# The gated channel stage rewritten: keys of two token blocks by seven products, streamed key weights, transposed outputs

## The chip, the cores and the metric

One core of a Trainium2 chip runs the whole program. The metric is the device time of one execution in microseconds, as the median of repeated runs. The engines are TensorE (PE, with its weight loads as PEld), VectorE (DVE), ScalarE (ACT), GpSimd (POOL), and SyncE (SP), which issues all DMAs here. Each engine takes its instructions in program order.

## The reference

Eight batches of 576 tokens; eight heads of width 64. A retention layer (causal, with decay per head) feeds a channel mixer with a low-rank mix over the sequence, and its result feeds a second mixer, the gated stage, which the change rewrites:

```python
x = retention(q, k, v)                      # (8, 576, 512)
u = x + (x.T @ U @ V).T
x = u + np.maximum(u @ w_ch1, 0) @ w_ch2    # 512 -> 2048 -> 512
x_prev = shift_by_one_token(x)
xk = mu_k * x + (1 - mu_k) * x_prev
xr = mu_r * x + (1 - mu_r) * x_prev
k = np.maximum(xk @ w_k, 0.0)               # 512 -> 1024
v = k * k @ w_v                             # 1024 -> 512
out = v / (1 + np.exp(-(xr @ w_r)))
```

## The kernel before

Channels lie on partitions and tokens on the free axis, in 9 blocks of 512 tokens (`BT`). Every fp32 product is made of three fp32r matmuls: operands are split into a high part (a cast on ACT) and a low part (a subtraction), and high x high, low x high and high x low are summed in PSUM. A matmul is 128x128 stationary by 128x512 moving unless said otherwise.

The program has five stages. (1) Retention in 72 steps (`step_of`), with the first projection's tiles (`hidden`, `hidden_part`, L233) filled in between. Weights arrive as float64 words and are converted by lists of small steps (`convert`, `park`, `second_weight`); `slot` takes one step of each conversion under way and starts a new one where told, so these lists set where conversions stand in the queues of ACT, DVE, POOL and SP. The weights of the last stage are parked in DRAM. (2) The rest of the first projection; its results go to DRAM. (3) The second projection of blocks 0 to 7, in pairs (`products`, L405): 64 items, each loaded, summed (L345 to L350) and split (`split_item`, L364 and L365) one item ahead, 24 matmuls in the first half of a pair's items and 18 in the second. Two token blocks and four quarters of the weight are combined by seven products for eight. The converted weight `w2p`/`w2q` of item j must be there at item j. (4) The second projection of block 8 (`project`, L485 to L487), with the weights of the last stage fetched meanwhile. (5) The gated stage, L1048 on.

Up to stage 4 the order is written by hand (`tc.manual_schedule`, left at L1045). The gated stage is left to the scheduler, which takes `pump`'s background steps at a lower priority. It goes block by block: `shift_mix` makes xk and xr and splits them (16 shifts on ACT, L524; a mix on DVE, L533; a cast, L537; a subtraction, L539); `key_chunk` (8 per block, 12 matmuls each) evicts with a ReLU on ACT, squares on DVE from PSUM (L1067), casts (L1068) and subtracts on POOL (L1069); `gate_tile` (4 of 12) ends in a sigmoid on ACT (L1084); `value_tile` (4 of 24) has tokens on the output's partitions, is multiplied by the gate (L1099) and stored (L1101). `wk`, `wr` and `wv` stay in SBUF.

```python
    for t in range(NB):
        ...
        for f in range(DF2 // 128):
            key_chunk(t, f)
            pump(5)
        for i in range(4):
            gate_tile(t, i)
            pump(5)
        pump(1000)
        ...
        for i in range(4):
            value_tile(t, i)
            pump(6)
```

## Time and profile before

| | |
|---|---|
| median of 3 runs | 1406.4 us (1406.31 to 1408.29) |
| the profiled execution, its own time | 1404.54 us |
| its span in the profile | 1402.8 us |
| PE busy in the span | 1378.8 us, 98% |
| granted clock of TensorE, mean | 0.991 |
| DVE / ACT / POOL busy | 53% / 41% / 23% |
| moved by DMA | 244.67 MB, mean 174 GB/s |
| share of the chain that ended last: keys L1061, values L1095, gates L1080 | 14%, 14%, 7% |

The span is what the profiler's records cover; the time of an execution is 1.7 us longer. Ends of matmuls are modelled and overlap, so a busy PE is read together with the spacing of its matmuls in the chain. Some matmul records are missing, so counts come from the program.

### The profile page before, as it was taken

Reading aid. Unit: us, or ns where it says so; the run is one execution under the profiler, and the core shown is the slowest. Engines: PE = TensorE matmul, PEld = TensorE weight load, DVE = VectorE, ACT = ScalarE, POOL = GpSimd, SP = SyncE. Lnnn points to the kernel's source line nnn. Section 1 sums busy time; section 2 is a strip of 40 time slices with the busy share of each in tenths; the row PEclk is TensorE's granted clock in tenths of the full one; section 3 lists DMA queues with packets and bytes.
Section 4 is the critical chain, followed back from the end, with each engine's and each line's share of the span. In section 5 each row is a group of like instructions: output and inputs, shape, how many; then the busy total and the mean of one; then the engine's idle time right before and its main releaser. Section 6 shows DMA issues by size and latency. Waiting matters only on the chain.

```text
span 1402.8 us, 25526 instructions
## 1 busy us (share of the span) xinstructions
PE 1378.8 (98%) x10332; PEld 1122.2 (80%) x10332; DVE 741.2 (53%) x1145; ACT 580.5 (41%) x1019; POOL 325.3 (23%) x263
## 2 busy tenths in 40 slices
PE   6899999999999999999999999999999999999998
PEld 4677778777788887788888888888888888888887
DVE  5873545444451467798898976425324234234240
ACT  4542333333332445344444443434444344344440
POOL 3350221211220255022222222031121120120220
PEclk8899999999999999999999999999999999999999
DMA  9757576676752658779696967921011011010000
GB/s 344 257 201 236 189 277 237 226 268 208 260 189 110 218 187 288 260 234 323 220 314 217 313 238 234 393 78 61 23 38 61 16 45 61 16 46 30 8 23 30
DMA packets 98950, 244.67 MB, mean 174 GB/s; under 512 B 12816, under 2 KB 19344, under 8 KB 98832
## 3 DMA queue, kind: packets, MB, share of 16 engines
q1 hardware_dynamic: 98832, 243.04, 50.6%
q8 instruction: 81, 1.33, 0.4%
q14 instruction: 37, 0.30, 0.1%
HBM read 158.07 MB, written 84.93 MB: 173 GB/s over the span
## 4 chain that ended last, share of the span: by engine, by line
PE 96%; DVE 2%; DMA 1%; issue 1%; ACT 0%; SPq 0%; DVEq 0%; ACTq 0%
PE h L233 29%; PE k L1061 14%; PE v L1095 14%; PE r L1080 7%; PE gc L405 6%; PE ga L405 6%; PE gd L405 6%; PE gb L405 3%; PE up L605 2%; PE xn L705 2%; PE dn L658 1%; PE c L487 1%; PE c L486 1%; PE c L485 1%; PE up L630 1%; PE dn L646 1%
## 5 line engine op out<-in xcount | busy, mean ns | idle before, releaser
L239 ACT ACTIVATE hs<-h 128x512 f32<-128x512 f32 x144 | 86.0, 598 | 242.9 <-PE h L233 238.2
L1069 POOL TENSOR_TENSOR kl<-ks,kh 128x512 fp32r<-128x512 f32 x72 | 92.8, 1290 | 359.2 <-issue 241.9
L1099 DVE TENSOR_TENSOR o<-v,g 128x512 f32<-128x512 f32 x36 | 24.9, 692 | 187.2 <-PE v L1095 187.2
L1067 DVE SCALAR_TENSOR_TENSOR ks<-k,ka 128x512 f32<-128x512 f32 x72 | 49.6, 691 | 122.7 <-ACT ka L1065 67.7
L364 ACT CAST sbh<-rb 128x1024 fp32r<-128x1024 f32 x64 | 67.4, 1053 | 68.4 <-PE gd L405 56.5
L537 ACT CAST mh<-m 128x512 fp32r<-128x512 f32 x72 | 44.8, 622 | 118.4 <-DVE tp L530 82.7
L1095 PE MATMUL v<-wv_0u,kh 128*128 128x512 f32 x288 | 88.7, 389 | 0.0
L1095 PE MATMUL v<-wv_1u,kh 128*128 128x512 f32 x288 | 88.7, 389 | 0.0
L617 DVE TENSOR_TENSOR pm<-up,dtab 128x256 f32<-128x256 f32 x72 | 30.4, 422 | 108.5 <-PE up L630 91.4
L365 DVE TENSOR_TENSOR sbl<-rb,sbh 128x1024 fp32r<-128x1024 f32 x64 | 86.4, 1350 | 2.4 <-ACT sbh L364 2.2
L365 DVE TENSOR_TENSOR sal<-ra,sah 128x1024 fp32r<-128x1024 f32 (+1 forms) x64 | 67.1, 1048 | 24.5 <-PE gd L405 16.5
L364 ACT CAST sah<-ra 128x1024 fp32r<-128x1024 f32 (+1 forms) x64 | 53.5, 837 | 49.7 <-DVE ra L346 22.9
L1080 PE MATMUL r<-wru,mh 128*128 128x512 f32 x288 | 71.4, 389 | 0.0
L1061 PE MATMUL k<-mh,wk_0u 128*128 128x512 f32 x288 | 71.4, 389 | 0.0
L1061 PE MATMUL k<-mh,wk_1u 128*128 128x512 f32 x288 | 71.1, 389 | 0.0
L1068 ACT CAST kh<-ks 128x512 fp32r<-128x512 f32 x72 | 44.5, 621 | 55.5 <-DVE ks L1067 55.5
L1065 ACT ACTIVATE ka<-k 128x512 f32<-128x512 f32 x72 | 43.1, 598 | 50.6 <-PE k L1061 41.6
L1080 PEld LDWEIGHTS r<-wru,mh 128*128 128x128 f32 x288 | 54.0, 188 | 11.6 <-ACT g L1084 0.5
L1061 PEld LDWEIGHTS k<-mh,wk_0u 128*128 128x128 f32 x288 | 54.0, 188 | 11.4 <-DVE ks L1067 0.2
L1095 PEld LDWEIGHTS v<-wv_0u,kh 128*128 128x128 f32 x288 | 54.1, 188 | 11.3
L1061 PEld LDWEIGHTS k<-mh,wk_1u 128*128 128x128 f32 x288 | 54.1, 188 | 11.2
L1095 PEld LDWEIGHTS v<-wv_1u,kh 128*128 128x128 f32 x288 | 54.0, 188 | 11.2
(196 smaller groups left out, 3327.7 us busy)
## 6 DMA issues: line engine op xcount, KB each, us to landing
hp<-hs SPq DMA_DIRECT2D x128, 256.0 KB, 3.0
rb<-hp SPq DMA_DIRECT2D x64, 512.0 KB, 5.8
qk<-in_qk SPq DMA_DIRECT2D x32, 512.0 KB, 4.6
kv<-in_kv SPq DMA_DIRECT2D x32, 512.0 KB, 5.9
ra<-hp SPq DMA_DIRECT2D x32, 512.0 KB, 6.9
ur<-ub SPq DMA_DIRECT2D x18, 512.0 KB, 6.2
x2l<-xb SPq DMA_DIRECT2D x18, 512.0 KB, 5.2
out<-o SPq DMA_DIRECT2D x36, 256.0 KB, 2.0
```

Source lines behind the costliest of these rows:

```text
L233: nc.tensor.matmul(hps[t, f], w.part(lo, k, fo), u[k // 2][:, k % 2, :], start=(part == 0 and k == 0), stop=(part == 2 and k == KD - 1),)
L239: nc.scalar.activation(h, hps.pop((t, f)), AF.Relu)
L364: nc.scalar.copy(hi_, src)
L365: nc.vector.tensor_tensor(lo_, src, hi_.bitcast(F32), op=ALU.subtract)
L405: nc.tensor.matmul(group[g][p], l[:, col(p)], r, start=(h == 0 and j == 0 and i == 0), stop=(i == 2 and last), skip_group_check=True,)
L537: nc.scalar.copy(hk, m)
L1061: nc.tensor.matmul(ps, w.part(lo, k, fo), u[k // 2][:, k % 2, :], start=(i == 0), stop=(i == len(ops) - 1))
L1067: nc.vector.scalar_tensor_tensor(sq, ps, 0.0, a, op0=ALU.max, op1=ALU.mult)
L1068: nc.scalar.copy(kh, sq)
L1069: nc.gpsimd.tensor_tensor(kl, sq, kh.bitcast(F32), op=ALU.subtract)
L1080: nc.tensor.matmul(ps, x[k // 2][:, k % 2, io_], wr.part(lo, k), start=(j == 0), stop=(j == len(ops) - 1))
L1095: nc.tensor.matmul(ps, x[:, f % 2, io_], wv[f // 4].part(lo, f % 4), start=(j == 0), stop=(j == len(ops) - 1))
```

## The change

The gated stage goes by pairs of blocks (0 and 1, 2 and 3, 4 and 5, 6 and 7), block 8 alone, inside the hand order. What moves:

- *Keys by seven products.* For a pair and each of four groups g, the key weight's columns g and g+4 (of 8 tiles of 128), each in two halves of the 512 channels, form A11, A12, A21, A22, and the two blocks' halves X11, X21, X12, X22. `key_group` computes A11 X11, S3 T3, S1 T1, A12 X21, S2 T2, A22 T4, S4 X22 in four PSUM banks a, c, d, b, a, c, d: the last three accumulate onto the first, third and second bank after ACT has copied what stood there.
- *Key weights.* `key_weight` replaces the parks of `wk`: it forms S1 to S4 on POOL, splits all eight quarters and stores 2 MB per group. `load_keys` fetches a group (4 DMAs of 512 KB) ahead of its use, anew for every pair.
- *Preparation.* `prepare(q)` replaces `shift_mix`: xr of both blocks, then the seven X and T tiles with their splits. It is pumped three steps at a time in six value parts and eight gate tiles of the pairs' turn, six at a time in stage 4.
- *Transposed outputs, values per key group.* `value_part` adds one group's two tiles into four banks with output channels on partitions; the kernel's output is (512, 4608) and is transposed on the host. Gates are transposed too and held.
- *Elsewhere.* Two steps of retention (c of 4, batches 2 and 3) now take two hidden tiles instead of one; the last `second_weight` waits in `tick` and is started by `slot(2)` in the item loop; `SMALL` is 9, `cf` has 5 buffers.

```diff
@@ key_weight, new; load_keys, new
+        def sums():
...
+            nc.gpsimd.tensor_tensor(s1, a21, a22, op=ALU.add)
+            nc.gpsimd.tensor_tensor(s2, s1, a11, op=ALU.subtract)
+            nc.gpsimd.tensor_tensor(s3, a11, a21, op=ALU.subtract)
+            nc.gpsimd.tensor_tensor(s4, a12, s2, op=ALU.subtract)
...
+        return [
+            load, None, down, lambda: fill(0), lambda: fill(1), sums, lambda: parts(0),
+            lambda: store(0), lambda: parts(1), lambda: store(1),
+        ]
...
+    def load_keys(n):
+        for i, w in enumerate((wkp, wkq)):
+            w[n] = []
+            for lo in range(2):
+                x = big.tile([128, 4, 256], F32R, tag="unit", name=f"wk{n}_{i}{lo}")
+                nc.sync.dma_start(x.bitcast(F32), kept_k[n % NG][:, i, lo])
+                w[n].append(x)
@@ prepare, new; shift_mix goes
+        def split(nm, src):
...
+            nc.scalar.copy(h, src)
             yield
+            nc.vector.tensor_tensor(l, src, h.bitcast(F32), op=ALU.subtract)
             yield
...
+            yield from split("22", b[1])
...
+            nc.vector.tensor_tensor(t3, b[1], b[0], op=ALU.subtract)
             yield
+            yield from split("t3", t3)
+            nc.vector.tensor_tensor(b[0], b[0], a[0], op=ALU.subtract)
+            yield
+            yield from split("t1", b[0])
+            nc.vector.tensor_tensor(b[1], b[1], b[0], op=ALU.subtract)
+            yield
+            yield from split("t2", b[1])
+        yield from half(ts[0], 1)
+        yield from split("21", a[1])
+        if len(ts) == 2:
+            nc.vector.tensor_tensor(a[1], a[1], b[1], op=ALU.subtract)
+            yield
+            yield from split("t4", a[1])
@@ in the loops
+        for g in range(NG):
+            waiting.insert(4 * g, key_weight(g, big))
...
-            hidden(2 if b > 1 and c not in (4, 7) and i > 2 * NL + 1 else 1, False)
+            few = i < 2 * NL + 2 or c == 7 or c == 4 and b > 3
+            hidden(1 if few else 2, False)
...
-        slot(new=len(ticks) % 4 == 1)
+        slot(new=len(ticks) % 4 == 1 and len(waiting) > 1)
...
-        if waiting or going:
-            tick()
+        if n:
+            slot(2)
@@ square and key_group, new
+    def square(t, g, i, x, eng):
...
+        nc.vector.scalar_tensor_tensor(x, x, 0.0, x, op0=ALU.max, op1=ALU.mult)
+        nc.scalar.copy(h, x)
+        eng.tensor_tensor(l, x, h.bitcast(F32), op=ALU.subtract)
...
+        for m in (1, 7, 5, 2, 6, 4, 3):
...
+            if m in (1, 7, 5, 6):
+                kept[m] = small(F32, f"m{m}_{n}")
+                nc.scalar.copy(kept[m], ps[b])
+            elif m == 2:
+                nc.vector.tensor_tensor(kept[1], ps[b], kept[1], op=ALU.add)
+                square(te, g, 0, kept[1], nc.gpsimd)
+                nc.vector.tensor_tensor(kept[7], kept[7], kept[5], op=ALU.add)
+            else:
+                t, i = ((te, 1), (to, 0))[m == 3]
+                x = small(F32, f"c{m}_{n}")
+                nc.vector.tensor_tensor(x, ps[b], kept[6], op=ALU.add)
+                square(t, g, i, x, nc.gpsimd)
+                if m == 3:
+                    nc.vector.tensor_tensor(kept[7], kept[7], kept[6], op=ALU.add)
+                    square(to, g, 1, kept[7], nc.gpsimd)
@@ the stage's loop, new (a pair)
+            for o in range(KD):
+                gate_tile(t, o, (mine, other)[x])
+                pump(3)
...
+        pump(1000)
...
+            for g in range(NG):
+                n = q * NG + g
+                if g + 1 < NG:
+                    load_keys(n + 1)
...
+                key_group(n, mine)
+                if g > 0:
+                    if g == NG - 1:
...
+                        load_keys(n + 1)
+                        background.append(prepare(q + 1))
+                        PUMP[0] = 3
+                    value_part(ts[0], g - 1, other)
+            value_part(ts[0], NG - 1, other)
+            for g in range(NG):
+                value_part(ts[1], g, mine)
```

Three places in the programs, row by row. First DVE at the entry of stage 3, before: `w2f7`, `w2p7` and `w2q7` belong to the last weight's conversion, `rb`/`ra` are an item's sums, `sal` and `sbl` its splits (with ACT's casts `sah`, `sbh`).

```order
L281 TENSOR_SCALAR w2f7_6947<-w2a7_6924 128x512
L284 SCALAR_TENSOR_TENSOR w2f7_6947<-w2a7_6924,w2f7_6947 128x512
L287 SCALAR_TENSOR_TENSOR w2f7_6947<-w2raw7_1_6873,w2f7_6947 128x512
L365 TENSOR_TENSOR sbl0_6978<-rb0_6849,sbh0_6977 128x1024
L365 TENSOR_TENSOR sal0_6982<-ra0_6848,sah0_6981 128x1024
L345 TENSOR_TENSOR rb1_6897<-rb1_6897,ra1_6896 128x512
L346 TENSOR_TENSOR ra1_6896<-ra1_6896 128x512
L315 TENSOR_TENSOR w2p7_1_7030<-w2f7_6947,w2p7_0_7029 128x512
L315 TENSOR_TENSOR w2q7_1_7032<-w2f7_6947,w2q7_0_7031 128x512
L345 TENSOR_TENSOR rb2_6952<-rb2_6952,ra2_6951 128x512
L346 TENSOR_TENSOR ra2_6951<-ra2_6951 128x512
L365 TENSOR_TENSOR sal1_7049<-ra1_6896,sah1_7048 128x1024
```

All of it stands ahead of the sums and splits of items 1 and 2. The same conversion in the change, three items later:

```order
L457 TENSOR_TENSOR sal3_7182<-ra3_7057,sah3_7181 128x1024
L457 TENSOR_TENSOR sbl3_7186<-rb3_7058,sbh3_7185 128x1024
L373 TENSOR_SCALAR w2f7_7216<-w2a7_7213 128x512
L376 SCALAR_TENSOR_TENSOR w2f7_7216<-w2a7_7213,w2f7_7216 128x512
L379 SCALAR_TENSOR_TENSOR w2f7_7216<-w2raw7_0_7170,w2f7_7216 128x512
L437 TENSOR_TENSOR rb5_7132<-rb5_7132,ra5_7131 128x512
L438 TENSOR_TENSOR ra5_7131<-ra5_7131 128x512
L457 TENSOR_TENSOR sal4_7228<-ra4_7084,sah4_7227 128x1024
L457 TENSOR_TENSOR sbl4_7232<-rb4_7085,sbh4_7231 128x1024
L373 TENSOR_SCALAR w2f7_7216<-w2a7_7213 128x512
L376 SCALAR_TENSOR_TENSOR w2f7_7216<-w2a7_7213,w2f7_7216 128x512
L379 SCALAR_TENSOR_TENSOR w2f7_7216<-w2raw7_1_7172,w2f7_7216 128x512
```

The first of its three groups now stands between the split of item 3 and the sums of item 5, the second between the split of item 4 and the sums of item 6; the subtractions follow behind the split of item 5. Item 1 has none of it ahead.

Second, PE at the turn to block 1, before: whole key chunks `k`, twelve matmuls per output tile.

```order
L1061 MATMUL k1_0_10354<-mh1_0_0_10192,wk_0u00_9641 128x512 x2
L1061 MATMUL k1_0_10354<-mh1_0_1_10193,wk_0u10_9645 128x512 x2
L1061 MATMUL k1_0_10354<-mh1_0_0_10192,wk_0u01_9643 128x512 x2
L1061 MATMUL k1_0_10354<-mh1_0_1_10193,wk_0u11_9647 128x512 x2
L1061 MATMUL k1_0_10354<-ml1_0_0_10194,wk_0u00_9641 128x512 x2
L1061 MATMUL k1_0_10354<-ml1_0_1_10195,wk_0u10_9645 128x512 x2
L1061 MATMUL k1_1_10373<-mh1_0_0_10192,wk_0u00_9641 128x512 x2
L1061 MATMUL k1_1_10373<-mh1_0_1_10193,wk_0u10_9645 128x512 x2
```

And in the change at the turn to the second pair: `ka` and `kc` are banks of group 4 (the first of that pair), `wk4` its streamed weights.

```order
L1207 MATMUL ka4_11035<-kh11_1_10812,wk4_00_10586 128x512
L1207 MATMUL ka4_11035<-kh11_1_10812,wk4_01_10588 128x512
L1207 MATMUL ka4_11035<-kl11_1_10813,wk4_00_10586 128x512
L1207 MATMUL ka4_11035<-kh11_1_10812,wk4_00_10586 128x512
L1207 MATMUL ka4_11035<-kh11_1_10812,wk4_01_10588 128x512
L1207 MATMUL ka4_11035<-kl11_1_10813,wk4_00_10586 128x512
L1207 MATMUL kc4_11037<-kht3_1_10907,wk4_00_10586 128x512
L1207 MATMUL kc4_11037<-kht3_1_10907,wk4_01_10588 128x512
L1207 MATMUL kc4_11037<-klt3_1_10908,wk4_00_10586 128x512
L1207 MATMUL kc4_11037<-kht3_1_10907,wk4_00_10586 128x512
L1207 MATMUL kc4_11037<-kht3_1_10907,wk4_01_10588 128x512
L1207 MATMUL kc4_11037<-klt3_1_10908,wk4_00_10586 128x512
```

A product has six matmuls, and the bank `ka` is used again four products later.

Third, DVE at that turn, before: the last mixes and splits of block 1 and the first squares `ks` of its key chunks.

```order
L530 MEMSET tp1_1_2_10332 128x1
L533 SCALAR_TENSOR_TENSOR m1_1_2_10336<-x2l1_1_9941,mu_93,tp1_1_2_10332 128x512
L530 MEMSET tp1_1_3_10340 128x1
L533 SCALAR_TENSOR_TENSOR m1_1_3_10344<-x2l1_1_9941,mu_93,tp1_1_3_10340 128x512
L539 TENSOR_TENSOR ml1_1_1_10287<-m1_1_2_10336,mh1_1_1_10285 128x512
L539 TENSOR_TENSOR ml1_1_1_10287<-m1_1_3_10344,mh1_1_1_10285 128x512
L1067 SCALAR_TENSOR_TENSOR ks1_0_10369<-k1_0_10354,ka1_0_10367 128x512
L1067 SCALAR_TENSOR_TENSOR ks1_1_10388<-k1_1_10373,ka1_1_10386 128x512
```

In the change, the end of the pair's preparation and the start of its first key group (`x2l2`, `x2l3` are blocks 2 and 3, mixed in place; `klt2`, `kl21`, `klt4` low parts; `m1`, `m7`, `c4` what ACT or DVE took from the banks):

```order
L648 TENSOR_TENSOR klt2_1_10947<-x2l3_1_10292,kht2_1_10946 128x1024
L616 MEMSET tp2_0_2_10965 128x1
L620 SCALAR_TENSOR_TENSOR x2l2_1_10288<-x2l2_1_10288,mu_97,tp2_0_2_10965 128x512
L616 MEMSET tp2_0_3_10984 128x1
L620 SCALAR_TENSOR_TENSOR x2l2_1_10288<-x2l2_1_10288,mu_97,tp2_0_3_10984 128x512
L648 TENSOR_TENSOR kl21_1_10990<-x2l2_1_10288,kh21_1_10989 128x1024
L680 TENSOR_TENSOR x2l2_1_10288<-x2l2_1_10288,x2l3_1_10292 128x1024
L648 TENSOR_TENSOR klt4_1_11010<-x2l2_1_10288,kht4_1_11009 128x1024
L1215 TENSOR_TENSOR m1_4_11045<-kb4_11036,m1_4_11045 128x512
L1186 SCALAR_TENSOR_TENSOR m1_4_11045<-m1_4_11045 128x512
L1217 TENSOR_TENSOR m7_4_11053<-m7_4_11053,m5_4_11061 128x512
L1221 TENSOR_TENSOR c4_4_11090<-kc4_11037,m6_4_11082 128x512
```

The first group's additions and squares stand directly behind the split of T4 in DVE's queue.

## Rows read from the trace of the kernel before

**Rows 1.** The page, part 1: busy time, share and instructions by engine.

```profile
PE 1378.8 (98%) x10332; PEld 1122.2 (80%) x10332; DVE 741.2 (53%) x1145; ACT 580.5 (41%) x1019; POOL 325.3 (23%) x263
```

**Rows 2.** Busy time by stretch: us, engines, PEclk, DMA share, GB/s.

```profile
424.60:492.50 67.90, 67.90 (x413) 55.51 (x410) 23.33 (x39) 27.22 (x50) 12.57 (x13) 1.00 0.49 169
552.00:620.00 68.00, 64.31 (x275) 52.20 (x275) 57.21 (x60) 31.28 (x42) 19.12 (x12) 0.97 0.72 239
864.70:916.00 51.30, 51.30 (x227) 42.19 (x226) 23.67 (x35) 17.79 (x30) 8.88 (x7) 1.00 0.91 328
916.00:1400.00 484.00, 482.83 (x2129) 399.00 (x2127) 164.77 (x295) 199.45 (x371) 93.34 (x75) 1.00 0.11 37
```

**Rows 3.** The chain that ended last, 480 to 920 us: start, us, what.

```profile
479.92 71.64 PE h L233 x316
...
907.26 3.40 PE k L1061 x15
```

**Rows 4.** Waits of PE: in total, times, longest us.

```profile
PE ga L405 <- DVE sal L365: 4.4, 4, 3.2
...
PE gb L405 <- DVE sbl L365: 0.5, 1, 0.5
```

**Rows 5.** The chain, 552 to 575 us.

```profile
553.31 1.68 DVE sal L365
560.27 2.30 DVE sal L365
562.61 2.07 PE ga L405 x4
564.68 1.83 PE gc L405 x6
```

**Rows 6.** Timeline of DVE, 536 to 580 us: start, us, instruction, idle before.

```profile
550.30 0.42 DVE L281 TENSOR_SCALAR w2f<-w2a 128x512 uint32<-128x512 uint32 x1
550.75 0.69 DVE L284 SCALAR_TENSOR_TENSOR w2f<-w2a,w2f 128x512 uint32<-128x512 uint32 x1
...
560.27 2.29 DVE L365 TENSOR_TENSOR sal<-ra,sah 128x1024 fp32r<-128x1024 f32 x1
...
566.08 1.22 DVE L365 TENSOR_TENSOR sal<-ra,sah 128x1024 fp32r<-128x1024 f32 x1
```

**Rows 7.** Timeline of POOL, 530 to 600 us.

```profile
534.63 1.29 POOL L315 TENSOR_TENSOR w2p<-w2s,w2p 128x512 fp32r<-128x512 f32 x1 [3.62 <-ACT w2p L314]
...
561.43 2.25 POOL L315 TENSOR_TENSOR w2q<-w2s,w2q 128x512 fp32r<-128x512 f32 x1
```

**Rows 8.** DMA issues, 900 to 1400 us, then 400 to 560: KB, us to landing.

```profile
x2l<-xb SPq DMA_DIRECT2D x16, 512.0 KB, 5.2
wv_1u<-wv_kept SPq DMA_DIRECT2D x3, 512.0 KB, 10.6
...
w2raw<-in_moe_w_ch SPq DMA_DIRECT2D x16, 512.0 KB, 4.7
```

**Rows 9.** Groups of ACT: count, busy us, mean ns, idle before, releaser.

```profile
L364 ACT CAST sbh<-rb 128x1024 fp32r<-128x1024 f32 x64 | 67.4, 1053 | 68.4 <-PE gd L405 56.5 <-DMA ra<-t 3.6 <-PE ga L405 2.9
L524 ACT ACTIVATE tp<-x2l,omu 128x511 f32<-128x511 f32 x72 | 51.5, 715 | 5.6 <-DMA x2l<-xb 5.6
L537 ACT CAST mh<-m 128x512 fp32r<-128x512 f32 x72 | 44.8, 622 | 118.4 <-DVE tp L530 82.7 <-DVE m L533 30.3 <-PE c L487 5.2
...
L1084 ACT ACTIVATE g<-r 128x512 f32<-128x512 f32 x36 | 21.5, 597 | 61.0 <-PE r L1080 60.9
...
L526 ACT ACTIVATE tp<-edge,omu 128x1 f32<-128x1 f32 x64 | 17.9, 279 | 0.0
```

**Rows 10.** Groups of POOL.

```profile
L1069 POOL TENSOR_TENSOR kl<-ks,kh 128x512 fp32r<-128x512 f32 x72 | 92.8, 1290 | 359.2 <-issue 241.9 <-ACT kh L1068 117.3
...
L296 POOL TENSOR_TENSOR w2s<-w2f 128x256 f32<-128x256 f32 x8 | 6.8, 850 | 41.1 <-DVE w2f L287 41.1
```

**Rows 11.** Groups of DVE.

```profile
L533 DVE SCALAR_TENSOR_TENSOR m<-x2l,mu,tp 128x512 f32<-128x512 f32 x72 | 53.7, 751 | 13.5 <-ACT tp L524 6.5
L1067 DVE SCALAR_TENSOR_TENSOR ks<-k,ka 128x512 f32<-128x512 f32 x72 | 49.6, 691 | 122.7 <-ACT ka L1065 67.7 <-POOL kl L1069 54.9
...
L1099 DVE TENSOR_TENSOR o<-v,g 128x512 f32<-128x512 f32 x36 | 24.9, 692 | 187.2 <-PE v L1095 187.2
```

**Rows 12.** Timeline, 1398 to 1403 us: the end.

```profile
1399.00 0.69 DVE L1099 TENSOR_TENSOR o<-v,g 128x512 f32<-128x512 f32 x1 [4.79 <-PE v L1095]
```

More of the change, by code (lines that the diff above doesn't have):

```diff
@@ new lines, in key_tile @@
+    def key_tile(t, g, i, b):
+        n = NB // 2 * NG + g
+        w = (wkp, wkq)[i][n]
+        ps = bank(b, f"k{t}_{g}_{i}")
+        ops = [(k, l, r) for k in range(KD) for l, r in ((0, 0), (1, 0), (0, 1))]
+        for j, (k, l, r) in enumerate(ops):
+            x = xk[NB // 2, ("11", "21")[k // 2]]
+            nc.tensor.matmul(
+                ps, w[l][:, k // 2, col(k % 2)], x[r][:, k % 2, :],
+                start=(j == 0), stop=(j == len(ops) - 1),
+            )
+        a = small(F32, f"ka{g}_{i}")
+        nc.scalar.copy(a, ps)
+        square(t, g, i, a, nc.vector)
@@ new lines, in value_part @@
+    def value_part(t, g, base):
+        if g == 0:
+            vacc[t] = [bank(base + o, f"v{t}_{o}") for o in range(KD)]
+        kh, kl = kk.pop((t, g))
+        for i in range(2):
+            w = wv[i]
+            for o in range(KD):
+                for j, (lo, x) in enumerate(((0, kh), (1, kh), (0, kl))):
+                    nc.tensor.matmul(
+                        vacc[t][o], w.part(lo, g, col(o)), x[:, i, :],
+                        start=(g == 0 and i == 0 and j == 0),
+                        stop=(g == NG - 1 and i == 1 and j == 2),
+                    )
+            pump(PUMP[0])
+        if g == NG - 1:
+            for o in range(KD):
+                x = small(F32, f"o{t}_{o}")
+                nc.vector.tensor_tensor(x, vacc[t][o], gate[t, o // 2][:, o % 2, :], op=ALU.mult)
+                nc.sync.dma_start(io["out"][col(o), t * BT:(t + 1) * BT], x)
@@ L1029, in retention_mixer_kernel @@
         if p == 5:
-            load_u(NB - 1, big2)
-        if p == 1:
-            load_x2(0, big2)
-            background.append(shift_mix(0, 0, big))
-            background.append(shift_mix(0, 1, big))
-        for _ in range(2):
-            if p > 0 and fetches:
-                w, i = fetches.pop(0)
-                w.load(big, i)
-        pump(4)
-    finish(NB - 1)
-    while fetches:
-        w, i = fetches.pop(0)
-        w.load(big, i)
-    pump(1000)
-    order.__exit__(None, None, None)
```

292 lines of the change are left out of this document (193 added, 99 removed).

## The prediction

> **What bounds the kernel now.** I read the page's busy times first, then the windows by stage, then the chain, then the waits of PE. TensorE is busy 98% of the span [rows 1]. In the gated stage (916 to 1400 us) it is busy 482.8 of 484.0 us at a granted clock of 1.00, while DVE has work for 165, ACT for 199 and POOL for 93 us, and the DMA engines are used 11% [rows 2]. So a wait must show in PE itself to cost anything there, and whatever PE no longer computes is time. The chain prices one matmul: 316 of them in 71.64 us and 15 in 3.40 us, both 226.7 ns [rows 3]. PE's own longest wait since the start is at the entry of the second-projection stage: 3.2 us on DVE's split `sal` [rows 4]. The slice 552 to 620 is the only later one with PE visibly short of its time, 64.3 of 68.0 us at clock 0.97 [rows 2].
>
> **The matmuls.** Before, one block's gated stage is 96 key, 48 gate and 96 value matmuls. For a pair of blocks the keys are 192. After, a pair takes 4 groups x 7 products x 2 halves x 3 split terms = 168, as the order of PE shows (5436 matmuls of 128x512 before, 5340 now). Four pairs save 4 x 24 = 96 matmuls; gates, values and block 8 keep theirs. 96 x 226.7 ns = **21.8 us**, all of it on PE, which is the path [rows 2, 3]. The new matmuls have the same tile (128x128 stationary, 128x512 moving) so I take the same price.
> The Trainium skill (TensorE: Matmul & The Clock Gate, section Back-to-back issue gap) puts a sustained stream of weight load and matmul at about 131 ns for 512 columns. By that figure the 96 would be worth an estimated 12.6 us and the time would be some 9 us above my forecast; the rows of this case do not agree with it, and the sum goes by them.
>
> **The moved weight conversion.** `second_weight(7)` used to be converted just ahead of the first product; now its three DVE groups stand behind the splits of items 3, 4 and 5. Before, this crowd cost PE 0.5 + 3.2 us of waiting, and after the wait 4 matmuls took 2.07 and 6 took 1.83 us where 0.91 and 1.36 are the rule [rows 4, 5]: 1.6 us more, 5.3 in all. Without the conversion's 0.4 + 0.7 + 0.7 us (twice, [rows 6]) and its two subtractions, `sal` of item 1 comes some 4 us earlier and the old wait is nearly gone. But the work is paid later: an item's products last 24 x 0.2267 = 5.4 us, DVE's own part of an item is 2 x 0.69 + 2 x 1.22 = 3.8 us, so 1.6 us is free per item, and the conversion needs 5.0 us plus what POOL's share of it slows: a split of 1.22 us took 2.29 while POOL subtracted, and POOL's 1.29 became 2.25 [rows 6, 7]. Its raw weights are also read later, behind the item loads (4.7 us to landing [rows 8]), and ACT and DVE stand still in order until they are there. The bounds are 5.3 us saved and, if the same crowd waits twice, 5.3 lost. I take **1.0 saved**, since the free time of items 3 to 6 (6.5 us) is about what the conversion and its slowing need.
>
> **Key weights, converted and streamed.** Before, `wk` is converted by 8 parks; now by 4 key conversions: as many DVE groups, 8 more casts on ACT (0.62 us each), 16 sums (0.85) and 8 more subtractions (1.29) on POOL [rows 9, 10]. They lie beside the recurrence and the first projection, where the slice of the same kind of conversion shows PE busy 67.9 of 67.9 us [rows 2]. I take 0; if the cover went, one wait like the longest on record, 3 us. In the gated stage each group fetches 4 x 512 KB, issued one group ahead: 2 MB against 9.5 us of products (14.9 with a value part). At the 328 GB/s of the slice 864.7 to 916 [rows 2] that is 6.4 us; 512 KB landed in 5.2 us singly and 10.6 in a crowd [rows 8]. Cost 0; at the far end 10.6 - 9.5 = 1.1 us at the first group of four pairs, 4.4 us. At the stage's entry 12 loads (6.3 MB, 19 us) are queued after the last projection, and the second group's key is due 21.8 + 9.5 = 31 us later: hidden.
>
> **Preparation of the next pair.** This is the one place where PE can be made to wait on a chain. `prepare(q+1)` starts behind key group 3, is spread over six value parts and eight gate tiles (240 matmuls, 54.4 us), and its last piece, T4, is due at the sixth product, 30 matmuls or 6.8 us later. ACT needs 16 x (0.715 + 0.279) + 8 x 0.622 + 7 x 1.053 = 28.3 us, DVE 16 x 0.75 + 8 x 0.69 + 11 x 1.22 = 30.9 [rows 6, 9, 11]; 8 sigmoids (4.8) and 8 output products (5.5) share the queues. Each engine alone fits easily. But the end (split 22, T3, T1, T2, split 21, T4) hands one tile to and fro: sum 1.22, cast 1.05, split 1.22, four times 3.5 and twice 2.3, plus two mixes: 21 us without gaps, some 24 with the sigmoids that fall into it. It begins behind the first gate tile (2.7 us) and its sigmoid (0.6), so ACT copies the first key product, behind it in its queue, at about 27.5; PE reuses that bank 21.8 + 5.4 = 27.2 us after the gate tiles began. I take **0.5 us for each of three pairs, 1.5**. The first pair's preparation has seven projection steps as well, and block 8 has no pair.
>
> **Key groups among themselves.** ACT copies four products (0.6 each), DVE does nine operations of 0.69, POOL four of 1.29 per group [rows 9 to 11]: 6.2 and 5.2 us beside 9.5. The last product of a group ends at 9.5; its bank is read by 10.5 and overwritten at 12.2 by the next group. Margin 1.7, cost 0.
>
> **The end.** Last matmul, one product of 0.69 us, one store [rows 12]. Now four stores come 0.68 us apart, each 256 KB, which at 328 GB/s needs 0.80: **0.4 us** more.
>
> **Sum**, against the profiled execution's own 1404.5 us: -21.8 - 1.0 + 1.5 + 0.4 = -20.9, giving 1383.6. The median of the runs shown is 1406.4, 1.9 above that execution, so the forecast is **1385.5 us**. What a measurement of this kernel can tell from no change is about 0.2%, 2.8 us.
>
> **The rivals.**
> A. *The late conversion costs nothing*: the DVE lead of items 1 to 3 swallows it. For it: 1.6 us free per item. Against: POOL's slowing. 5.3 saved in place of 1.0: 1381.2.
> B. *The key weights come late* at the first group of each pair, as in the crowd of 10.6 us [rows 8]. Against: only 11% DMA use in that stage. 4.4 us: 1389.9.
> C. *DVE and POOL exclude each other* inside the key groups. For it: 2.29 and 2.25 us side by side against 1.22 and 1.29 alone [rows 6, 7]; before, the squares of this stage ran at 0.69 because they read PSUM [rows 11], while four squares a group now read SBUF twice. Two blockings of 1.29 in a group exceed the margin of 1.7 by 0.9; 16 groups give 14 us: 1399.9. Against: the bank reads themselves keep one PSUM source.
> The Trainium skill (SBUF — State Buffer, section Who interferes with whom) states that a DVE instruction with two SBUF inputs and a GpSimd one that reads SBUF exclude each other for a whole instruction. By that rule the squares wait and the bank reads do so only behind them; the rows at 560 us agree with it.
> D. *Slower*: the preparation chain of a pair runs with no overlap between ACT and DVE. Then 28.3 + 30.9 + 4.8 + 5.5 = 69.5 us must pass in 54.4 + 6.8 = 61.2: 8.3 us of PE waiting at the first key group of three pairs, each followed by the 1.6 us of slow matmuls seen after a wait [rows 5]. 3 x 9.9 = 29.7 in place of 1.5: 1413.7, slower by 0.5%. It decides from about 5.7 us of wait per pair upward. For it: one generator, each step needing the last; against: for the first half (the eight gate splits) the next shift runs on ACT while DVE subtracts, so overlap is built in.
>
> **How the numbers follow.** Forecast 0.70 (its own range 1381 to 1392), A 0.08, B 0.07, C 0.07, D 0.08. Of D about a quarter is a half-exposed chain that lands within 2.8 us of before. So faster 0.92, same 0.02, slower 0.06. The range goes from 1380, just under A, to 1397, above B and over the half of C where fewer groups are blocked; D and the worst of C are left out, some 12 in 100, the rest being uncertainty within the forecast (the 5.3 us lost, the 3 us of the early stage).
>
> **What would show it.** Right: 96 fewer matmul records of 128x512, 226.7 ns apart; a gated stage some 21 us shorter with PE waits under 3 us in it; the waits on `sal` no longer at item 1 but small ones at items 4 to 6; the first key product of pairs 1 to 3 waiting about half a microsecond on ACT. Wrong: PE waiting for `wk` loads (B), DVE squares of 1.3 us or more and waits at bank d (C), waits of 5 us and more with a lower granted clock at three places 103 us apart (D), or a matmul spacing other than 226.7 ns.

## The result and the profile after

The changed kernel takes 1394.55 us (median of 4 runs, 1392.13 to 1395.8) beside 1406.45 us for the kernel before (1406.31 to 1408.29): a ratio of 0.991 with a 95% interval of 0.9893 to 0.9927, so 11.9 us faster. The forecast was 1385.5 us, 20.9 us faster, in a range of 1380 to 1397. The sign is right and the time lies in the range, near its upper end: 9 us of the expected gain are missing.

The page of the changed kernel, part 1, answers to [rows 1]: 96 matmuls fewer, as counted, while DVE has gained 115 us of work and is still far from PE.

```profile
span 1393.3 us, 25624 instructions
...
PE 1359.9 (98%) x10236; PEld 1103.6 (79%) x10236; DVE 856.2 (61%) x1243; ACT 589.1 (42%) x1021; POOL 353.2 (25%) x279
```

The time of PE between points that both programs share tells where it went. The points are the fifth transpose `xn` of the retention stage (called the recurrence from here on), the first product of the second projection (`ga` to `gd`), the first gate matmul, the last matmul. All are starts on PE's timeline, in us; 36 key matmuls of the kernel before lie ahead of its first gate matmul, and their 8.2 us (36 x 226.7 ns) are counted in the gated stage.

| stretch | before | after | difference | the prediction's term |
|---|---|---|---|---|
| start to fifth `xn` | 36.1 | 38.6 | +2.5 | 1.9 (own time against median) |
| fifth `xn` to first product | 516.2 | 523.1 | **+6.9** | 0, at most 3 |
| first product to first gate | 356.4 | 355.5 | -0.9 | -1.0 |
| gated stage to last matmul | 489.8 | 471.5 | **-18.3** | -21.8 + 1.5 |
| last matmul to the end | 4.3 | 4.7 | +0.4 | +0.4 |
| span | 1402.8 | 1393.3 | -9.4 | -20.9 |

Two lines are off: the recurrence lost 6.9 us where nothing was forecast, and the gated stage won 2.0 us less than forecast. Both show in PE's own waits, which answer to [rows 4].

```profile
PE xn L850 <- ACT xs L860: 5.0, 3, 1.8
...
PE ga L497 <- DVE sal L457: 3.4, 3, 2.1
PE ka L1207 <- ACT m L1213: 2.7, 4, 0.7
```

**In the recurrence** PE now waits three times for ACT's eviction `xs`, in chunks 3, 4 and 5. (The 72 steps go through eight sequences of nine steps and five transposes each; these are the chunks, numbered from 0.) In the kernel before PE is busy through the whole of such a stretch. The busy times by stretch, first of the kernel before, then of the changed kernel for the two chunks and for the stretches that answer to [rows 2]; the columns are those named there.

```profile
190.00:250.00 60.00, 60.00 (x806) 47.94 (x806) 28.40 (x57) 21.46 (x41) 12.15 (x11) 1.00 0.70 243
250.00:310.00 60.00, 60.00 (x806) 47.91 (x806) 28.39 (x57) 21.46 (x41) 12.14 (x11) 1.00 0.69 234
```

```profile
200.00:262.00 62.00, 60.38 (x806) 47.99 (x805) 28.48 (x60) 23.71 (x45) 19.06 (x18) 1.00 0.79 268
262.00:323.00 61.00, 59.41 (x802) 47.19 (x801) 27.55 (x60) 23.69 (x45) 18.10 (x17) 1.00 0.80 268
561.70:630.00 68.30, 64.86 (x281) 52.01 (x280) 61.80 (x64) 32.53 (x43) 22.57 (x14) 1.00 0.76 255
917.20:1388.90 471.70, 469.04 (x2065) 386.96 (x2063) 280.57 (x379) 196.67 (x351) 98.24 (x68) 1.00 0.37 130
```

PE lacks 1.6 us in each of the two chunks, at a DMA share of 0.79 and 0.80 instead of 0.70 and 0.69. DVE has no more work than before, ACT 2 us more and POOL 6 to 7 us more. The timelines of SP, ACT and PE around the first of these waits show what is late.

```profile
188.00 1.40 SPq L275 DMA_DIRECT2D keys<-wkl  x2
194.63 0.33 SPq L712 DMA_DIRECT2D qk<-in_qk  x1
...
197.94 1.16 SPq L179 DMA_DIRECT2D wr_raw<-in_moe_w_r  x1
```

```profile
205.47 0.66 ACT L104 ACTIVATE ca<-wr_raw 128x512 f32<-128x512 f32 x1 [7.45 <-DMA wr_raw<-in_moe_w_r]
206.04 0.57 ACT L860 COPY xs<-xn 128x512 f32<-128x512 f32 x1
```

```profile
204.62 0.41 PE L803 MATMUL dn<-pm,kv 64*64 64x64 f32 x16
206.66 0.63 PE L850 MATMUL xn<-ident,xt 128*64 128x128 f32 x4 [1.62 <-ACT xs L860]
```

Behind the key stores SP issues nothing from 189.4 to 194.6 us. In the trace the second of these stores, asked for at 187.18 us, lands at 194.56, and the load of `qk` is asked for at 194.63; the last one lands at 195.81, and the load of `kv` is asked for at 195.87. The raw weight that is queued behind is asked for at 197.9 and lands at 205.4; ACT, whose queue says to scale it now, stands 7.45 us; the eviction behind it is late, and PE waits. SP's waits in 200 to 323 us name what held it: buffers whose stores had not landed. In 190 to 310 us of the kernel before SP has no such wait on a store.

```profile
SPq L712 <- DMA keys<-wkh: 11.3, 2, 6.4
SPq L712 <- DMA wv_kept<-wv_0p: 3.5, 1, 3.5
SPq L714 <- DMA wr_kept<-wrp: 2.9, 1, 2.9
```

**In the gated stage** 96 gate matmuls run from 917.21 to 938.97 us, 226.7 ns each, as forecast. The only waits are the four of 0.7 us at `ka`, one in each pair. With the restart behind it each loses 0.9 to 1.0 us. They stand not at the first key group, where the preparation ends, but at the sixth product (the fifth in the order of issue) of the second key group. The first pair around that place, on PE, ACT, DVE and POOL:

```profile
953.70 0.39 PE L1207 MATMUL kb<-kl,wk 128*128 128x512 f32 x1
954.83 0.73 PE L1207 MATMUL ka<-kht,wk 128*128 128x512 f32 x2 [0.74 <-ACT m L1213]
```

```profile
950.27 0.62 ACT L1187 CAST vh<-c 128x512 fp32r<-128x512 f32 x1 [0.70 <-DVE c L1186]
953.67 0.62 ACT L1187 CAST vh<-m 128x512 fp32r<-128x512 f32 x1 [2.77 <-DVE m L1186]
954.20 0.58 ACT L1213 COPY m<-ka 128x512 f32<-128x512 f32 x1
```

```profile
949.55 0.69 DVE L1186 SCALAR_TENSOR_TENSOR c<-c 128x512 f32<-128x512 f32 x1
950.16 1.78 DVE L1224 TENSOR_TENSOR m<-m,m 128x512 f32<-128x512 f32 x1
951.98 1.66 DVE L1186 SCALAR_TENSOR_TENSOR m<-m 128x512 f32<-128x512 f32 x1
```

```profile
949.65 3.45 POOL L1188 TENSOR_TENSOR vl<-c,vh 128x512 fp32r<-128x512 f32 x2 [1.47 <-ACT vh L1187]
```

While POOL makes its two subtractions DVE's last sum and square of the group take 1.78 and 1.66 us instead of 0.69, so ACT's cast of that square comes late, and behind it in ACT's queue stands the copy of the next group's first product, which frees bank a for that group's sixth product. All subtractions of this kind beside DVE (`vl<-c`) and the others (`vl<-m`), from the page, with their mean in ns:

```profile
L1188 POOL TENSOR_TENSOR vl<-m,vh 128x512 fp32r<-128x512 f32 x32 | 41.4, 1293 | 266.0 <-ACT vh L1187 241.1
L1188 POOL TENSOR_TENSOR vl<-c,vh 128x512 fp32r<-128x512 f32 x32 | 55.2, 1745 | 24.7 <-ACT vh L1187 24.7
```

In the later groups a value part of 5.4 us lies between, and nothing waits.

### The profile page after: what moved, and what is told of

Read it like the earlier page. It is cut to its first block, busy times and chain, and to the rows that moved or that the text cites. A ratio compares the mean times of both kernels' runs of the same rounds, so it can differ in the third digit from the quotient of the medians.

```text
span 1393.3 us, 25624 instructions
## 1 busy us (share of the span) xinstructions
PE 1359.9 (98%) x10236; PEld 1103.6 (79%) x10236; DVE 856.2 (61%) x1243; ACT 589.1 (42%) x1021; POOL 353.2 (25%) x279
## 4 chain that ended last, share of the span: by engine, by line
PE 85%; DVE 6%; DMA 6%; issue 2%; ACT 1%; SPq 0%; DVEq 0%; ACTq 0%
PE h L325 28%; PE v L1252 14%; PE r L1174 7%; PE gc L497 4%; PE gd L497 4%; PE ga L497 4%; PE ka L1207 3%; PE kc L1207 3%; PE kd L1207 3%; PE gb L497 2%; PE up L750 2%; PE k L1236 2%; PE kb L1207 2%; DVE sal L457 1%; PE xn L850 1%
## 5 line engine op out<-in xcount | busy, mean ns | idle before, releaser
L1174 PE MATMUL r<-rh,wru 128*128 128x512 f32 x288 | 88.6, 389 | 0.0
L1252 PE MATMUL v<-vh,wv_0u 128*128 128x512 f32 x288 | 88.6, 389 | 0.0
L1252 PE MATMUL v<-vh,wv_1u 128*128 128x512 f32 x288 | 88.6, 389 | 0.0
L1174 PEld LDWEIGHTS r<-rh,wru 128*128 128x128 f32 x288 | 54.1, 188 | 11.2
L1252 PEld LDWEIGHTS v<-vh,wv_0u 128*128 128x128 f32 x288 | 54.1, 188 | 11.2
L1252 PEld LDWEIGHTS v<-vh,wv_1u 128*128 128x128 f32 x288 | 54.1, 188 | 11.2
L1188 POOL TENSOR_TENSOR vl<-c,vh 128x512 fp32r<-128x512 f32 x32 | 55.2, 1745 | 24.7 <-ACT vh L1187 24.7
L1174 PE MATMUL r<-rl,wru 128*128 128x512 f32 x144 | 56.0, 389 | 0.0
L1252 PE MATMUL v<-vl,wv_0u 128*128 128x512 f32 x144 | 56.0, 389 | 0.0
L1252 PE MATMUL v<-vl,wv_1u 128*128 128x512 f32 x144 | 56.0, 389 | 0.0
```

Of the source, the lines that this page charges most:

```text
L1174: nc.tensor.matmul(ps, wr.part(lo, k, col(o)), x[k // 2][:, k % 2, :], start=(j == 0), stop=(j == len(ops) - 1),)
L1188: eng.tensor_tensor(l, x, h.bitcast(F32), op=ALU.subtract)
L1252: nc.tensor.matmul(vacc[t][o], w.part(lo, g, col(o)), x[:, i, :], start=(g == 0 and i == 0 and j == 0), stop=(g == NG - 1 and i == 1 and j ...
```

## The experiments

In the table the profiled execution of each kernel is cut at the same points. The middle columns are the recurrence from the fifth transpose to the first product, then the second projection, then the gated stage.

| kernel | median us | ratio, 95% interval | to fifth `xn` | to first product | to first gate | to last matmul |
|---|---|---|---|---|---|---|
| changed kernel | 1394.55 | 0.9893-0.9927 | 38.6 | 523.1 | 355.5 | 471.5 |
| late_down | 1394.89 | 0.9900-0.9925 | 38.2 | 522.9 | 355.9 | 471.5 |
| sum_early | 1394.62 | 0.9884-0.9912 | 38.8 | 526.4 | 355.7 | 469.1 |
| old_ticks | 1399.60 | 0.9933-0.9968 | 38.4 | 525.4 | 359.3 | 471.5 |
| one_store | 1393.95 | 0.9892-0.9917 | 38.9 | 521.9 | 355.8 | 471.6 |
| no_store | 1386.80 | 0.9844-0.9871 | 39.0 | 517.2 | 355.2 | 469.1 |
| keys_gap | 1386.91 | 0.9843-0.9870 | 37.3 | 518.5 | 355.2 | 469.1 |
| keys_late | 1405.80 | 0.9989-1.0006 | 38.8 | 535.5 | 356.5 | 469.5 |
| gap_only | 1389.75 | 0.9861-0.9891 | 38.6 | 518.0 | 356.3 | 471.5 |
| gap_old | 1391.59 | 0.9877-0.9906 | 39.5 | 519.7 | 359.3 | 469.1 |
| gap_spread | 1389.42 | 0.9856-0.9891 | 39.0 | 519.5 | 355.0 | 469.1 |
| bytes_only | 1386.61 | 0.9831-0.9873 | 36.9 | 518.4 | 356.0 | 469.1 |

**late_down: an empty slot ahead of ACT's scaling.**

```diff
-                waiting.append(convert(fetch, parts, 128, 512, store))
+                steps = convert(fetch, parts, 128, 512, store)
+                steps.insert(1, None)
+                waiting.append(steps)
```

> Edit: the conversion of each parked weight (`wr`, `wv`) gets one empty slot between the load of the raw words and ACT's scaling of them. Theory (ACT reads its queue in order and stands behind raw weights that SP, busy with the key stores, asks for late; the evictions `xs` behind it make PE wait 1.8 us at three places): the three waits of xn on xs, 5.0 us together, and their restarts go, the first product of the second projection comes some 5 us earlier, and the time is 1389 to 1391. Rival (the early loss comes from the other spread of the hidden first-projection tiles, two at step 4 of the first chunks): no change, 1393 to 1396. Rival (the load is simply too slow for any slot): the wait of ACT moves to the next slot, with another instruction behind it, and the time stays within 2 us of 1394.5.

No change in the time. The waits on `xs` at the transposes are gone, 5.0 us of them, but PE lost as much in other places: from the last transpose of chunk 3 to that of chunk 4 it takes 61.8 us, as the changed kernel does (59.9 before). Its waits between 140 and 335 us:

```profile
PE dn L793 <- POOL kv L723: 2.1, 2, 1.1
PE mx L903 <- ACT xs L862: 0.7, 3, 0.2
PE h L327 <- ACT hs L333: 0.2, 1, 0.2
```

So ACT's place in line was a symptom. With it out of the way PE waits for POOL's `kv`, the load of the next chunk; these waits are 3.0 us, and how the rest of the loss comes about was not taken apart. The time is also what the first rival forecast, the other spread of the hidden tiles; that rival falls with no_store, bytes_only and keys_gap below, which keep this spread and lose 1.0 to 2.4 us in the recurrence instead of 6.9.

**sum_early: the last sum and square of a key group made earlier.**

```diff
                 nc.scalar.copy(kept[m], ps[b])
+                if m == 6:
+                    nc.vector.tensor_tensor(kept[7], kept[7], kept[6], op=ALU.add)
+                    square(to, g, 1, kept[7], nc.gpsimd)
...
-                if m == 3:
-                    nc.vector.tensor_tensor(kept[7], kept[7], kept[6], op=ALU.add)
-                    square(to, g, 1, kept[7], nc.gpsimd)
```

> Edit: in a key group the seventh product's last sum and its square are made behind product 6 instead of last, so that the last square of a group is that of product 3. Theory (the four waits of 0.7 us at the sixth product of the second group of each pair come from ACT's copies standing behind the cast of the last square, which DVE makes in 1.8 + 1.7 us instead of 0.7 + 0.7 while POOL subtracts): these waits, 2.7 us, and the 0.3 us lost at each restart go, 3 to 4 us faster, 1390.5 to 1391.5. Rival (they are the end of the preparation chain, as forecast): the waits stay at pairs 2 to 4 and the time changes by less than 1 us.

The four waits on `ka` are gone, and the gated stage is 2.4 us shorter. Its profile has only one group of waits left from 560 us on:

```profile
PE ga L497 <- DVE sal L457: 4.1, 5, 2.0
```

Of the 0.9 to 1.0 us per pair 0.3 to 0.4 stay: by the spacing of the matmuls PE now loses them one product later, at bank c. The time did not follow in this pair of medians, because the recurrence, where the program is the same as in the changed kernel, took 526.4 us here and 523.1 there; the runs of this kernel spread from 1389.99 to 1396.49 us. keys_gap against gap_only, below, gives the same edit a time: 1386.91 against 1389.75, 2.8 us. The rival (the end of the preparation chain) falls: nothing of that chain was touched, and the wait stood in the first pair too.

**old_ticks: the last weight pair converted ahead of the first products again.**

```diff
-        slot(new=len(ticks) % 4 == 1 and len(waiting) > 1)
+        slot(new=len(ticks) % 4 == 1)
...
-        if n:
-            slot(2)
+        if waiting or going:
+            tick()
```

> Edit: the slots around the second projection as before the change (a new conversion at every fourth tick, ticks and not pairs of slots in the item loop), so that `second_weight(7)` is converted ahead of the first products again. By the prediction's term (moved conversion, 1.0 us saved) this is 1.0 us slower than the changed kernel, 1395 to 1396; the wait on `sal` at item 1 is back at some 3 us. Rival A (the late conversion costs nothing): 4 to 5 us slower, 1399. Rival (the same crowd waits twice, nothing saved): 0 to 4 us faster.

5.0 us slower, the time that rival A gave. Of it the second projection holds 3.8 us (359.3 against 355.5); the rest is the recurrence, which has the same program. To have the move without that noise it was repeated on keys_gap (gap_old).

**one_store: one DMA where two stored a part.**

```diff
-                for w in range(2):
-                    nc.sync.dma_start(
-                        kept_k[g][:, w, lo, 2 * i:2 * i + 2], x[:, 2 * w:2 * w + 2].bitcast(F32)
-                    )
+                nc.sync.dma_start(
+                    kept_k[g][:, :, lo, 2 * i:2 * i + 2],
+                    x.bitcast(F32).rearrange("p (w s) n -> p w s n", w=2),
+                )
```

> Edit: each part of the converted keys is stored by one DMA instead of two, 4 issues on SP per key group and not 8. Theory (SP's queue, crowded by the key stores of 0.6 to 0.7 us each, issues the raw weights late): the loads behind come 1.3 to 2.6 us sooner, the three waits on xs shrink by about half, 1 to 3 us faster, 1391.5 to 1393.5. Rival (the raw weights are late because SP waits for a store's data or a free buffer, and the number of issues is nothing): no change within 1 us, 1393.5 to 1395.5.

0.6 us, within the spread, and the waits on `xs` are 4.2 us in place of 5.0. The number of issues on SP is not it; the rival's time came.

**no_store and bytes_only: what of the store costs.** The first leaves the stores out, and the gated stage reads other words of the same number in their place; the second leaves the converted parts unstored and moves the same bytes from a table that holds no buffer of the conversions. Both have the early last sum.

```diff
-            lambda: store(0), lambda: parts(1), lambda: store(1),
+            None, lambda: parts(1),
...
-                nc.sync.dma_start(x.bitcast(F32), kept_k[n % NG][:, i, lo])
+                nc.sync.dma_start(
+                    x.bitcast(F32), wr.kept[:, :, lo, i * 256:(i + 1) * 256]
+                )
```

> Edit: the converted keys are not stored (this leaves out the 8.4 MB of key stores in the recurrence; the gated stage reads other words of the same number in their place), with the early last sum of sum_early in the gated stage. Theory (the chunks 3 to 5 of the recurrence lose some 1.8 us each because SP's loads of the next chunk wait for buffers whose key store has not landed, at a DMA share of 0.79 where it was 0.70 before, and ACT, DVE and POOL stand behind late loads): the waits of SP on key stores go, the DMA share of 200 to 330 us falls to about 0.72, PE waits for nothing there, and the first product of the second projection comes at 557 to 558 us, 5 us earlier; the time is 1385 to 1388. Rival (it is the arithmetic of the key conversion on ACT, DVE and POOL, 8 more casts, 16 sums and 8 more subtractions): the first product stays at 561 to 564 and the time at 1390 to 1392, the gain of the early sum alone.

```diff
-                        kept_k[g][:, w, lo, 2 * i:2 * i + 2], x[:, 2 * w:2 * w + 2].bitcast(F32)
+                        kept_k[g][:, w, lo, 2 * i:2 * i + 2],
+                        qtab[:, w].rearrange("p a i -> p (a i)").rearrange("p (s n) -> p s n", n=256)
```

> Edit: the key stores move the same bytes to the same places, but from a table that is always there (the factors of the queries) instead of from the converted parts, which this leaves unstored; so a part's buffers are free as soon as they are made. With the early last sum, to be set against no_store (no bytes, no buffers held) and sum_early (both). If the held buffers are the cause: first product of the second projection 517 to 519 us behind the fifth transpose, as in no_store (517.2), DMA share of 200 to 323 us still at 0.78 or more, time 1386 to 1388. If the bytes are the cause: 521 to 526 us, as in the changed kernel (523.1) and sum_early (526.4), PE waits on xs at chunks 3 to 5, time 1391 to 1395.

Both have the recurrence back: 517.2 and 518.4 us, where the kernel before takes 516.2 and the changed kernel 523.1. Busy times of the two chunks, first of no_store, then of bytes_only:

```profile
200.00:262.00 62.00, 62.00 (x814) 49.49 (x813) 29.39 (x60) 23.77 (x46) 20.60 (x19) 1.00 0.71 240
262.00:323.00 61.00, 61.00 (x810) 48.63 (x810) 30.71 (x66) 25.31 (x48) 19.22 (x17) 1.00 0.72 239
```

```profile
200.00:262.00 62.00, 62.00 (x814) 49.51 (x813) 27.76 (x61) 24.32 (x47) 18.60 (x17) 1.00 0.79 273
262.00:323.00 61.00, 60.79 (x808) 48.34 (x806) 27.99 (x63) 24.58 (x48) 18.60 (x17) 1.00 0.79 274
```

This separates the two things that were one in the theory. With all the bytes of the changed kernel on the DMA engines (0.79) PE waits for almost nothing, as long as no buffer is held by them. And the arithmetic of the conversion, still all there in both, costs PE 0.2 us at most in these two chunks. (bytes_only also frees the stores from waiting until a part is made; but in 200 to 323 us of the changed kernel SP's waits at its store line are 0.7 us in all, and none is for a part.) The loss is the time for which a converted part keeps its buffers until its store has landed, while SP's next load, in line, wants that buffer. What the 1.0 to 2.2 us are that stay above the kernel before was not taken apart.

**keys_gap, gap_only and keys_late: the same work, placed otherwise.** The first two leave a place of the sequence empty behind each key conversion (the first with the early last sum, the second without); the third puts the key conversions at places 9, 11, 13 and 15, with the early last sum.

```diff
-            waiting.insert(4 * g, key_weight(g, big))
+            waiting.insert(5 * g, key_weight(g, big))
+            waiting.insert(5 * g + 1, [None])
```

> Edit: behind each of the four key conversions in the recurrence one place of the sequence stays empty (two steps), so that the next raw weight is asked for later; with the early last sum. Theory (the crowd of bytes and buffers around each key conversion): the waits on xs shrink from 1.8 us to below 1 at each of three places, first product at 558 to 561, time 1387 to 1389.5. Rival (each key conversion costs its 1.8 us wherever it stands): first product at 562 to 566, time 1390 to 1392.

> Edit: the empty places behind the key conversions alone, without the early last sum. Theory (the two losses are separate: 5 to 6 us in the recurrence, 0.6 us a pair at the second key group): 2.4 us slower than keys_gap, 1389 to 1390, with the four waits on the copies of product 1 back and the gated stage at 471.5 us from first to last matmul. Rival (the early last sum gives nothing that shows in the time): 1386 to 1388.

Both as the theory said, keys_gap at the lower edge of its range: 518.5 and 518.0 us in the recurrence, and the waits of SP on stores in 200 to 323 us are gone. 1386.91 us is 7.6 us less than the changed kernel and 1.4 more than the forecast: it beats both kernels, at a ratio of 0.9857 to the kernel before. gap_only has the four waits back and 471.5 us of gated stage.

```diff
-            waiting.insert(4 * g, key_weight(g, big))
+            waiting.insert(8 + 2 * g, key_weight(g, big))
```

> Edit: the four key conversions stand at places 9, 11, 13 and 15 of the sequence instead of 1, 5, 9 and 13, so that they run in the last three chunks, where the DMA share of the changed kernel falls to 0.36; with the early last sum. Theory (bytes and buffers): the loss of chunks 3 and 4 goes, some is left where two conversions overlap in chunks 5 and 6; first product at 558 to 562, time 1386.5 to 1390. Rival (each key conversion costs 1.8 us wherever it stands): the loss only moves to the later chunks, first product at 562 to 566, time 1390 to 1392.

Both expectations fell: 1405.8 us, 11 us slower than the changed kernel. Chunks 3 and 4 are clean, as the theory had it, but from the last transpose of chunk 4 to that of chunk 5 it takes 70.3 us in place of 62.1, and from there to the last one of chunk 7 127.5 in place of 119.0. PE's two long waits in the timelines of DVE and PE, then the stretch of the first:

```profile
303.19 0.88 DVE L233 TENSOR_SCALAR wkf<-ca 128x512 uint32<-128x512 uint32 x1 [7.39 <-DMA keys<-wkl]
305.45 0.41 DVE L762 TENSOR_TENSOR pm<-up,dtab 128x256 f32<-128x256 f32 x1
306.30 0.70 PE L750 MATMUL up<-qk 64*64 64x64 f32 x16 [6.90 <-issue]
...
372.09 0.89 DVE L233 TENSOR_SCALAR wkf<-ca 128x512 uint32<-128x512 uint32 x1 [5.52 <-DMA keys<-wkl]
374.36 0.42 DVE L762 TENSOR_TENSOR pm<-up,dtab 128x256 f32<-128x256 f32 x1
375.20 0.70 PE L750 MATMUL up<-qk 64*64 64x64 f32 x16 [5.23 <-issue]
```

```profile
262.00:323.00 61.00, 53.30 (x657) 42.19 (x657) 26.77 (x54) 20.20 (x39) 17.73 (x17) 0.94 0.66 222
```

The same cause shows here on an engine itself. DVE stands 7.4 and 5.5 us at the first operation of a key conversion, whose tile `wkf` comes out of the same pool, until a store of the conversion before it has landed (in the trace at 303.00 and 371.97 us). Behind it in DVE's queue stand the operations that take the scores out of PSUM (`pm` and the next), and PE's next scores `up` start 0.8 us after `pm`. The profile names no releaser for PE there; that it waits for DVE is read from the order and the times. The DMA share of that stretch is only 0.66: a second sign that bytes are not the limit. With one raw weight between two key conversions, where the changed kernel has three, the second wants its tile while the stores of the first are under way.

**before_mem: the memory edits alone on the kernel before.**

```diff
-SMALL = 8
+SMALL = 9
...
-            f = got["f"] = cv.tile([128, 512], F32, tag="cf", name="cf", bufs=4)[:p, :n]
+            f = got["f"] = cv.tile([128, 512], F32, tag="cf", name="cf", bufs=5)[:p, :n]
...
-            vh = a2.tile([128, q], F32R, tag="vh", name="vh", bufs=1)
-            vl = a2.tile([128, q], F32R, tag="vl", name="vl", bufs=1)
+            vh, vl = small(F32R, "vh")[:, :q], small(F32R, "vl")[:, :q]
```

> Edit: the kernel before with the three changes of memory alone (nine small tiles, five `cf` tiles, `vh` and `vl` among the small tiles). Theory (the 2.4 us that all profiles of the changed kernel lose before 40 us come from no instruction, since the order of every engine is the same there, but from where the clock of PE rises again): the third transpose of the first chunk starts at 36 to 39 us and the time stays within 2 us of before, 1405 to 1409. Rival (the two small tiles hold up the first chunk): the third transpose starts at 38.5 us or later, and the time is 2 to 3 us longer, 1408.5 to 1410.

1407.39 us, a ratio of 1.0 (0.999 to 1.0009): the edits cost nothing. (The expectation says the third transpose; the figures that it gives are those of the fifth.) Yet its profile has the late start of the changed kernel. The fifth transpose in the kernel before, in this one and in the changed kernel:

```profile
36.14 0.63 PE L705 MATMUL xn<-ident,xt 128*64 128x128 f32 x4
```

```profile
38.46 0.63 PE L705 MATMUL xn<-ident,xt 128*64 128x128 f32 x4
```

```profile
38.59 0.58 PE L850 MATMUL xn<-ident,xt 128*64 128x128 f32 x2
```

In this run the recurrence takes 516.8 us, so the memory edits have no part in the 6.9 us either. So the first 2.5 us of the table belong to the profiled execution of the kernel before, which was quick there, and not to the change; the prediction had allowed for 1.9 of it by its median.

**gap_old and gap_spread: the late conversion.** gap_old is keys_gap with the edit of old_ticks. gap_spread is keys_gap with this:

```diff
-            slot(2)
+            slot(2 if n in (3, 6) else 1)
```

> Edit: keys_gap with the slots around the second projection as before the change, so that the last weight pair is converted ahead of the first products. By the prediction's term (1.0 us saved by the move) 1387.5 to 1388.5. Rival A (5.3 us saved by the move): 1391.5 to 1392.5. What old_ticks showed from the last transpose of the recurrence to the first gate (471.1 us against 467.6): 1390 to 1391.

> Edit: keys_gap with the late conversion spread over six items instead of four: its raw words get two items to land and the three DVE groups stand in items 3, 4 and 6. Theory (the late conversion still costs what the waits on `sal` at items 3 to 5 show, 2.9 us in keys_gap, for ACT stood 7.4 us behind the raw words): waits on `sal` below 1 us, 1 to 2.5 us faster than keys_gap, 1384.5 to 1386. Rival (DVE has no room in these items wherever the pieces stand): the same waits at other items, 1386.5 to 1387.5.

gap_old: 4.7 us slower than keys_gap, 4.2 of it in the second projection (359.3 against 355.2), near rival A's 5.3, and the time is the one that this rival gave. PE's waits there are more than the kernel before had [rows 4]: a cast on ACT is late as well.

```profile
PE ga L497 <- DVE sal L457: 4.9, 4, 3.4
PE ga L497 <- ACT sah L456: 2.1, 1, 2.1
```

gap_spread: no gain. The second projection takes 355.0 us against 355.2, the time is 2.5 us longer with intervals that overlap, and the wait has only moved, as the rival said. (In keys_gap the waits on `sal` stand at items 4 to 6, counted from 0, and not at 3 to 5 as the expectation has it; here the longest stands at item 7.)

```profile
PE ga L497 <- DVE w2p L407: 2.7, 1, 2.7
PE gc L497 <- DVE sbl L457: 0.6, 2, 0.4
PE ga L497 <- DVE sal L457: 0.4, 1, 0.4
```

## Why the prediction was right, and where it was wrong

- **The matmuls, 21.8 us: right.** 96 fewer, 226.7 ns each in the new products as in the old. The figure of the Trainium skill that was weighed (TensorE: Matmul & The Clock Gate, section Back-to-back issue gap) would by the estimate there have made the gain 9 us smaller, which is what the time shows; but the spacing of 226.7 ns shows that it is not for that reason. The agreement of the sum is chance.
- **The moved conversion, 1.0 saved: the size came out (0.9), the account behind it did not.** Undone in the changed kernel it costs 3.8 to 4.2 us, not 1.0. In the order of the new kernel two more hidden tiles are computed in the recurrence, so fewer ticks are left ahead of the first products, and the old rule puts the conversion deeper into the crowd. That this is the reason is argued from the order and the waits, not shown. The small waits on `sal` stand at items 4 to 6 as forecast, 3.4 us in all.
- **"I take 0; if the cover went, one wait like the longest on record, 3 us": this step failed**, with the recurrence 6.9 us longer and, where no buffer is held, 1.0 to 2.2 (no_store, bytes_only). The term counted engine time (casts, sums, subtractions) under a cover that was read from the slice 424.6 to 492.5 us [rows 2]. That slice is behind the crowded part; the four key conversions run between some 117 and 374 us. The engine time was indeed hidden. What was not counted is what a conversion holds: two raw tiles, the filled one and four parts, with stores to land, where two parks held four tiles, in a pool that the loads of the recurrence rotate through. The prediction's own sentence, that an engine stands still in order until its words are there, was said of the second projection only.
- **The streamed keys, 0: right.** No PE wait on them; 512 KB lands in 5.7 us in the median, 10.8 at the longest, with 9.5 at hand. Rival B falls.
- **"0.5 us for each of three pairs, 1.5" failed in its place, and "margin 1.7, cost 0" in its size.** The preparation costs PE nothing: in pairs 2 to 4 ACT copies the first key product 25.1 us after the gate tiles began, and not at 27.5, with the bank used again at 27.2. (The prediction's chain of 21 us is 20.1 by its own terms, 4 x 3.5 + 2 x 2.3 + 1.5, which alone takes nearly all of that wait away.) The loss is 0.9 to 1.0 us in each of four pairs, 3.8 in all, between the first and second key group. It is 3.5 net, since some 0.4 us that the kernel before lost in its first gates are gone: 489.8 - 21.8 + 3.5 = 471.5. The margin was worked out with DVE at 0.69 us throughout; beside POOL's subtractions the last sum and square took 2.1 us more, which 1.7 does not cover.
- **Rival C had the right mechanism and the wrong count**: 4 places in 16, because a value part stands behind all groups but the first. It forecast 14 us, and 3.8 came. The rule cited there (the Trainium skill, SBUF — State Buffer, section Who interferes with whom) agrees with the trace: POOL's `vl<-c`, beside DVE, takes 1745 ns in the mean and its `vl<-m` 1293. Three operations of DVE and two of POOL last from 949.55 to 953.64 us, 4.1 us, where their durations alone (3 x 0.69 and 2 x 1.29) add up to 4.7: they go nearly one after the other.
- **The end, 0.4: right** (0.4). Rival D did not come: no wait as long as 1 us in the gated stage.

In sum: 6.9 us in the recurrence, 2.0 more than forecast in the gated stage and 0.1 in the second projection make the 9.0 us between forecast and time. That the time still lies in the range is partly luck: its upper end was set for rival B and half of rival C, and the early stage had been given 3 us at most.

## What to carry to other kernels

When work is moved under cover, price what it holds and not only what it computes: every buffer that a store keeps until it has landed can stop the next load in an in-order queue, or the next conversion on an engine, and what stands behind it stops in turn. The wait that shows (ACT's eviction here) may be only the last link, so take away the first one and see whether the wait merely moves; an empty place behind each of four conversions in a hand-written order was worth 4.8 us here. And a margin between engines that share work is to be taken with the slowed durations, not those of an engine alone.
